# A linear-recurrence layer feeding a top-2 mixture of attention experts: a planner that prefers the present tiling, full-width gate matmuls, corrected planner costs, and a last unit that ends in two groups of query tiles

## The chip, the cores and the metric

The kernel runs on one core of a Trainium2 chip. The metric is device time in microseconds for one execution. Three executions before the change took 398.37, 399.69 and 401.26 us; their median, 399.69 us, is the time before. The execution that was profiled took 402.58 us, and its span, from the first to the last instruction, is 400.8 us.

## The reference

There are two layers. The first is a linear recurrence over 4 batches, 8 heads, 768 positions and head width 48. For each head, with a state of 48 x 48 that starts at zero:

```
cur   = outer(u * k[t], v[t])
y[t]  = r[t] @ (state + cur)
state = w[t][:, None] * state + outer(k[t], v[t])
```

Its output, with the heads side by side, is x of shape 4 x 768 x 384. The second layer takes x through four attention experts of head width 64, of which each position uses the two with the largest gate logits:

```
logits = x @ w_gate                      # 4 experts
w      = softmax over the 2 largest      # others weigh 0
for e in experts:
    q, k, v = x @ wq[e], x @ wk[e], x @ wv[e]
    a   = causal softmax(q @ k.T / 8)
    out += w[:, e] * (a @ v @ wo[e])
```

Every expert is computed for every position, and the weight of an expert that was not chosen is zero. The sharp scores (wq and wk are drawn with a large factor) are why products of q and k are split into a high and a low part and computed in three matmuls.

## The kernel before, in words

The work is cut into 8 units: batch b (4) times half g of the sequence (2), so a unit is 384 positions, which are 3 tiles of 128. A unit has a recurrence part, written by rwkv, and an attention part, written by moe.

**Recurrence.** Two heads are processed together, so a unit has 4 head pairs. The sequence is cut into chunks of 64. For a pair, VectorE runs scans over the decays (suf, pre), products go to GpSimd or VectorE (kt, mr, uk, ur), TensorE transposes kt (ktp, three 128x128 transposes) and multiplies in quarters of its array: aps (24 matmuls of 64x64), ups (state increments), and yps (outputs). VectorE scans over the chunk states (ys), masks aps into am, and adds yps to xn. One pair's ux step (line 409 on ScalarE) adds the u term, as three ScalarE instructions of 48 columns for each head.

**Attention.** xn is transposed (xp) and split into xh and xl. proj writes queries and keys of two experts at once (tile pp), vproj values and gate logits (vp). scores writes the scores of one query tile i for the two experts of a pair ep (tile sp), with the causal mask added by small matmuls; then come a maximum on VectorE (mx, line 650), an exponential on ScalarE (a, line 652), transposes on TensorE (tp, line 666), copies to ATa and ATb, and attend multiplies by the values (yp, line 689). gather computes the gates (gg on VectorE, then four GpSimd instructions that split them in three bf16 parts, a transpose gp, a copy gT); weigh spreads them over rows by a matmul with sel (gb) and multiplies; project_out multiplies by wo (op, line 758), copies (ob) and stores.

**Tilings.** A matmul uses the whole array of 128x128 (ktp, xp, pp, vp, tp, op), quarters of it (aps, ups, yps: mode "q"), two halves by rows (sp, and gb: mode "r") or two halves by columns (yp, and gp: mode "h").

**Order.** Nothing is issued in the order in which it is written. Every piece goes to Plan.add with the engines that may run it and a cost for each, the tiles that it reads and writes, and a wish time (want: the unit's start plus progress plus an offset for its kind from the table OFF, or OFF0 for the first unit). Plan.order then simulates all engines and picks, for each, among the ready pieces the one with the smallest wish time, no later than SLACK = 125 ns after the earliest that could start. A matmul of another tiling than the last one is charged DRAIN = 100 ns. So costs and offsets alone set the order of each engine's instructions, and every engine then runs its list strictly in that order.

**PSUM.** Of 8 banks, the recurrence has two (tag rw), the attention tiles two (mo), and scores two double ones (sc), each wide enough for both experts of a query tile up to 512 keys, or for one expert of a longer one. In the last unit no recurrence is left, and mbank alternates between mo and rw (the flag spare). BUFS gives the number of buffers of each tile in SBUF; ob has 2. Line 798 adds matmuls on a constant tile (warm), 14 at the start and 80 to be put where TensorE has nothing else.

**The last unit's end.** Its second expert pair computes scores for query tiles 0, 1, 2 in turn (512, 640 and 768 keys), then attend over all three tiles, gather, weigh and project_out.

## Time and profile before

| | |
|---|---|
| median of 3 executions | 399.69 us |
| the profiled execution | 402.58 us |
| its span | 400.8 us |
| TensorE busy with matmuls | 378.7 us, 94% |
| VectorE busy | 310.2 us, 77% |
| ScalarE busy | 236.2 us, 59% |
| GpSimd busy | 141.0 us, 35% |
| mean granted TensorE clock | 0.986 |

Busy time is the time in which at least one instruction of the engine is under way; with pipelined matmuls a busy TensorE is not one at its peak. In the answers that are quoted below, PE is TensorE, PEld its weight loads, DVE VectorE, ACT ScalarE, POOL GpSimd and SP SyncE. A row of the timeline has the start in us, the length in us, the engine, the line, what it writes and reads, the shape and the count of instructions merged in it; in brackets stands how long the engine had been idle and what released it. An fp32 matmul (aps, ups, yps, yp) is recorded as two instructions. A row of a table by stages has the stage, its length, and for each engine the busy time with the count of instructions, then the granted TensorE clock (1.00 is full), the share of the DMA engines and GB/s.

### The profile page before, as it was taken

What the parts mean: (1) busy time and instruction counts of PE and PEld (TensorE: products, weight loads), DVE (VectorE), ACT (ScalarE), POOL (GpSimd) and SP (SyncE); (2) the same over time, 40 slices, a digit from 0 to 9 for tenths busy, and PEclk for the clock granted to TensorE, in tenths of its full rate; (3) what the DMA queues carried; (4) which work ended last, traced back from release to release, by engine and by line L of the source; (5) the groups of instructions that cost most, each with busy time, mean ns of one, the idle gap of its engine ahead of it and who ended that gap; (6) DMA issues with size and microseconds to landing.
All of it is one profiled execution on the core that took longest, in us unless ns stands there. A gap on an engine that the chain in (4) does not pass through costs nothing.

```text
span 400.8 us, 12723 instructions
## 1 busy us (share of the span) xinstructions
PE 378.7 (94%) x5228; PEld 289.9 (72%) x5238; DVE 310.2 (77%) x684; ACT 236.2 (59%) x672; POOL 141.0 (35%) x247
## 2 busy tenths in 40 slices
PE   8789999999999999999989999999999999999875
PEld 3465877788857688778848688788768877778553
DVE  7989988998998988888946897786987853474332
ACT  2564766845667575746746587557645644556532
POOL 4435555452344555532212436533424102011000
PEclk9999999999999999999989999999999999999979
DMA  7885353544425527055403534431302001001001
GB/s 259 333 294 185 120 168 109 189 135 137 148 76 158 180 83 222 12 186 177 122 1 117 142 103 131 168 122 61 106 16 61 2 2 61 2 0 61 2 0 59
DMA packets 18057, 45.17 MB, mean 113 GB/s; under 512 B 2000, under 2 KB 9424, under 8 KB 18000
## 3 DMA queue, kind: packets, MB, share of 16 engines
q1 hardware_dynamic: 18000, 44.37, 34.2%
q8 instruction: 41, 0.67, 0.7%
q14 instruction: 16, 0.13, 0.1%
HBM read 39.64 MB, written 4.72 MB: 111 GB/s over the span
## 4 chain that ended last, share of the span: by engine, by line
PE 70%; DVE 13%; ACT 8%; DMA 5%; issue 3%; POOL 0%; ACTq 0%; POOLq 0%; DVEq 0%
PE pp L548 11%; PE tp L666 10%; PE sp L636 9%; PE yp L689 8%; PE vp L571 5%; PE aps L435 5%; PE op L758 5%; PE yps L479 4%; ACT xn L409 3%; DVE mx L650 3%; ACT a L652 3%; DVE ys L457 2%; PE yps L482 2%; PE ups L449 2%; PE ktp L419 2%
## 5 line engine op out<-in xcount | busy, mean ns | idle before, releaser
L652 ACT ACTIVATE a<-sp,mx 128x128 f32<-128x128 f32 (+5 forms) x96 | 60.8, 636 | 37.4 <-DVE mx L650 29.9
L650 DVE TENSOR_REDUCE mx<-sp 128x1 f32<-128x128 f32 (+5 forms) x96 | 56.4, 615 | 18.3 <-PE sp L641 16.4
L666 PE MATMUL tp<-ident,a 128*128 128x128 f32 x336 | 59.6, 291 | 8.2 <-ACT a L652 4.4
L666 PEld LDWEIGHTS tp<-ident,a 128*128 128x128 f32 x336 | 38.1, 143 | 19.0 <-ACT a L652 7.3
L389 POOL TENSOR_TENSOR kt<-lt,suf 128x384 f32<-128x384 f32 x31 | 31.7, 1022 | 42.4 <-PE aps L435 20.7
L396 POOL TENSOR_TENSOR nat<-nat,u_sb 128x288 f32<-128x288 f32 x30 | 27.0, 901 | 49.9 <-DMA nat<-in_nat_dram 29.3
L409 ACT ACTIVATE xn<-nat,rk 128x48 f32<-128x48 f32 x138 | 34.5, 325 | 13.4 <-DVE rk L402 13.3
L226 ACT COPY ATa<-tp 128x512 f32<-128x512 f32 (+3 forms) x64 | 30.8, 486 | 18.5 <-PE tp L666 17.7
L689 PE MATMUL yp<-ATa,v_sb 128*64 128x384 f32 (+2 forms) x224 | 40.2, 476 | 0.2 <-DVE ATa L228 0.2
L548 PE MATMUL pp<-xh,wh_qk 128*128 128x384 f32 x96 | 38.3, 399 | 0.5 <-ACT ATa L226 0.2
L384 DVE TENSOR_TENSOR_SCAN pre<-lt,inv_pre 128x390 f32<-128x390 f32 x32 | 34.1, 1067 | 0.1
L457 DVE TENSOR_TENSOR_SCAN ys<-ust,wdec 112x384 f32<-112x384 f32 x32 | 32.3, 1011 | 1.4 <-ACT ust L226 0.8
L380 DVE TENSOR_TENSOR_SCAN suf<-lt,one_suf 128x390 f32<-128x390 f32 x32 | 32.0, 1004 | 1.8 <-DMA lt<-in_wkr_dram 1.2
L479 PE MATMUL yps<-ys,pre 64*64 64x48 f32 (+1 forms) x768 | 31.2, 262 | 1.5 <-DVE am L438 0.8
L548 PE MATMUL pp<-xh,wl_qk 128*128 128x384 f32 x96 | 32.3, 337 | 0.0
L548 PE MATMUL pp<-xl,wh_qk 128*128 128x384 f32 x96 | 32.3, 337 | 0.0
L391 POOL TENSOR_TENSOR pre<-lt,pre 128x384 f32<-128x384 f32 x21 | 22.2, 1056 | 27.1 <-DVE pre L384 13.6
L435 PEld LDWEIGHTS aps<-pre,kt 64*64 64x64 f32 x768 | 25.0, 134 | 7.4 <-issue 3.5
L435 PE MATMUL aps<-pre,kt 64*64 64x64 f32 x768 | 29.3, 222 | 0.9 <-ACT kts L226 0.4
L387 ACT COPY wdec<-suf 128x288 f32<-128x288 f32 x32 | 22.6, 706 | 12.4 <-DVE suf L380 7.9
L479 PEld LDWEIGHTS yps<-ys,pre 64*64 64x64 f32 (+1 forms) x768 | 21.3, 133 | 10.0 <-issue 3.7
L482 PE MATMUL yps<-vy,am 64*64 64x48 f32 x768 | 28.2, 219 | 0.0
(135 smaller groups left out, 938.5 us busy)
## 6 DMA issues: line engine op xcount, KB each, us to landing
lt<-in_wkr_dram SPq DMA_DIRECT2D x31, 579.5 KB, 4.2
nat<-in_nat_dram SPq DMA_DIRECT2D x32, 432.0 KB, 3.8
vy<-in_vY_dram SPq DMA_DIRECT2D x32, 144.0 KB, 2.6
out_dram<-ob SPq DMA_DIRECT2D x24, 192.0 KB, 1.9
w_qk<-in_wqk_dram SPq DMA_DIRECT2D x1, 768.0 KB, 8.2
w_vg<-in_wvg_dram SPq DMA_DIRECT2D x1, 390.0 KB, 8.8
lt<-in_wkr_dram SPq DMA_DIRECT2D x1, 384.0 KB, 5.3
w_o<-in_wo_dram SPq DMA_DIRECT2D x1, 384.0 KB, 8.4
```

The source lines that it names most:

```text
L384: plan.add("pre", {"DVE": t_scan(WB)}, lambda e, pre=pre, w_=w_: nc.vector.tensor_tensor_scan(flat(pre()), w_()[:, 0:WB - 1], flat(inv_pre ...
L409: nc.scalar.mul(xn()[:, i, o], v[:, i, :], rk()[:, i, h:h + 1])
L435: nc.tensor.matmul(a_[half(h), c * C:(c + 1) * C], k[half(h), c, :], m[half(h), c, 0:C], start=True, stop=True)
L457: plan.add("ys", {"DVE": t_scan(D * NX)}, lambda e, ys=ys, us=us, wd=wd: nc.vector.tensor_tensor_scan(flat(ys()[0:112]), flat(us[0:112]), ...
L479: nc.tensor.matmul(yps[h]()[half(q), o], pre()[r, c, 0:C], ys()[r, :, c], start=i == 0, stop=False)
L482: nc.tensor.matmul(yps[h]()[half(q), o], am()[half(h), c, :], vy()[half(h), c, :], start=False, stop=i == 2)
L548: nc.tensor.matmul(pp()[:, 0:384], w[:, qk, k, cs], x()[:, k, :], start=(k == j == 0), stop=(k == j == 2))
L636: nc.tensor.matmul(spv(x)[:, h, :], q()[p, t], flat(k())[p, o], start=j == 0, stop=j == 2 and h < np_ - 1)
L650: plan.add("max", {"DVE": t_dve(n)}, lambda e, x=x, mx=mx: nc.vector.tensor_reduce(mx(), spv(x), axis=AX.XY, op=ALU.max, negate=True), [sp ...
L652: plan.add("exp", {"ACT": t_exp(n)}, lambda e, x=x, y=y, mx=mx, a=a: nc.scalar.activation(a()[:, 0:n].rearrange("p (a n) -> p a n", a=np_) ...
L666: nc.tensor.transpose(tp()[:, j * 128:(j + 1) * 128], a()[:, (j0 + j) * 128:(j0 + j + 1) * 128], ident)
L689: nc.tensor.matmul(yp()[e * 64:e * 64 + 64, lo:384], v_sb[ep]()[:, j, e * 64:e * 64 + 64], at, start=(j == 0), stop=(j == nj - 1))
```

## The change

The change has six parts, all in one edit.

1. In Plan.order, for TensorE alone, a piece of the present tiling has its wish time lowered by STAY = 2.0 us when the next piece is chosen, and the search among candidates goes on until the wish time is more than STAY past the first one's.
2. The gate matmuls are padded to the whole array: sel, gT and the gate tile have 128 rows or columns in place of 36, gp and gb get no tiling mode of their own, and gather clears the padded tile with a GpSimd memset.
3. Costs that the planner uses are changed: a ux on ScalarE from 273 to 675 ns, two GpSimd steps of the gates from 1300 and 700 to 1440 and 875 ns, the GpSimd step of gather from 1000 to 1290 ns.
4. In the last unit (batch 3, second half) scores with up to 512 keys go to the two banks of the recurrence, one for each expert.
5. In the last unit the second expert pair takes its query tiles in the order 1, 0, 2; attend, gather, weigh run for tiles 0 and 1 first and then for tile 2, and project_out of a tile reads only its group.
6. ob has 3 buffers in place of 2, and the tables of offsets (OFF, OFF0, MV, LEAD, T0, T1) have new numbers throughout.

The diff, cut; of the tables only three lines are shown:

```diff
@@ Plan.order
-                        if t <= free[e]:
+                        if t <= free[e] and (e != "PE" or want > c[0][1] + STAY):
                             break
...
-                want, n, t = min((x[1], x[2], x[0]) for x in c if x[0] <= t0 + slack)
+                want, n, t = min((x[1] - (STAY if e == "PE" and ops[x[2]]["mode"] == tiling else 0.0), x[2], x[0])
+                                 for x in c if x[0] <= t0 + slack)
@@ rwkv_moe
+    GROWS, GCOLS, GMODE = 128, 128, (None, None)
...
-    sel = cst.tile([NG, 3 * E, HD], BF16, name="sel")
+    sel = cst.tile([128, 3 * E, HD], BF16, name="sel")
...
-                plan.add("ux", dict(prod(144), ACT=3 * t_act(48)) if UXA else prod(144), ux, [(na, 0), rk], [(xn, p, h)])
+                plan.add("ux", dict(prod(144), ACT=675) if UXA else prod(144), ux, [(na, 0), rk], [(xn, p, h)])
@@ scores
-            sps = [bank("sc", f"sp{n0}{ep}{i}{a}", whole=np_ == 2) for a in range(np_)]
+            free = spare[0] and np_ == 1
+            sps = [bank("rw" if free else "sc", f"sp{n0}{ep}{i}{a}", whole=free or np_ == 2) for a in range(2 if free else np_)]
@@ attend, gather, weigh
+        last = (b, g) == (B - 1, 1)
+
+        groups = [(0, 2), (2, 3)] if last else [(0, 3)]
+
+        def attend(ep, ATs, i0, i1):
+
+            yp = mbank(f"yp{n0}{ep}{i0}")
+            nj = 3 * g + i1
             for j in range(nj):
...
+                ia = max(i0, j - 3 * g)
+                lo, hi = ia * 128, i1 * 128
...
+                gf = gg()[:, t].rearrange("p i e -> p (i e)")
+                a, b, c = (g3()[:, x * 3 * E + i0 * E:x * 3 * E + i1 * E] for x in range(3))
+                if GCOLS > NG or i1 - i0 < 3:
+                    V.memset(g3(), 0.0)
...
+            plan.add("g4", {"POOL": 1290}, parts, [gg], [gg, g3])
+            plan.add("gp", {"PE": 60}, lambda e: nc.tensor.transpose(gp()[0:GROWS, 0:128], g3(), identb), [g3], [gp], mode=GMODE[0])
+            plan.add("gT", {"DVE": 131}, lambda e: nc.vector.tensor_copy(gT(), gp()[0:GROWS, 0:128]), [gp], [gT])
...
+            plan.add("gb", {"PE": 56 * (i1 - i0)}, mm, [gT], [gb], mode=GMODE[1])
@@ moe
-            for i in range(3):
+            for i in (1, 0, 2) if last and ep else range(3):
...
+        for x, (i0, i1) in enumerate(groups):
+            gT = gather(i0, i1)
+            for ep in range(2):
+                weigh(ep, yps[ep][x if ep else 0], gT, i0, i1, *outs[ep])
+            for i in range(i0, i1):
+                project_out(i, [o[1:] for o in outs], i0)
@@ tables
-MV = {0: 27.58, 1: 45.34}
+MV = {0: 27.66, 1: 46.39}
...
+STAY = 2.0
...
-T0, T1 = (17.33, 15.85)
+T0, T1 = (21.06, 16.77)
```

Three places show how the instructions move. The first is TensorE's list in the second unit's attention, where two head pairs of the third unit's recurrence are woven in. ktp are the transposes of kt, aps and ups quarter-array work of the recurrence, tp the transposes of exponentials, sp scores. Before:

```order
L419 MATMUL ktp_1716<-ident,kt_1622 128x128 x3
L435 MATMUL aps_1724<-pre_1652,kt_1622 64x64 x12
L666 MATMUL tp_1746<-ident,a_1712 128x128 x4
L666 MATMUL tp_1760<-ident,a_1721 128x128 x4
L449 MATMUL ups_1767<-nat_1259,kts_1738 64x48
```

After:

```order
L421 MATMUL ktp_1716<-ident,kt_1603 128x128 x3
L437 MATMUL aps_1721<-pre_1628,kt_1603 64x64 x12
L437 MATMUL aps_1746<-pre_1699,kt_1676 64x64 x12
L671 MATMUL tp_1763<-ident,a_1738 128x128 x4
L421 MATMUL ktp_1770<-ident,kt_1676 128x128 x3
L671 MATMUL tp_1782<-ident,a_1761 128x128 x4
L641 MATMUL sp_1796<-Kh_700,Qh_1423 128x320
```

Two quarter-array pieces now stand one behind the other, and three whole-array pieces behind them, where before whole and quarter pieces took turns.

The second place is TensorE at the program's end, between the scores of the last unit's second expert pair and its attention. Before, with sp_6491 the scores of query tile 2 (768 keys) of the second expert:

```order
L641 MATMUL sp_6491<-causal,idh 128x128
L666 MATMUL tp_6517<-ident,a_6513 128x128 x4
L666 MATMUL tp_6522<-ident,a_6513 128x128 x2
L666 MATMUL tp_6527<-ident,a_6515 128x128 x4
L666 MATMUL tp_6536<-ident,a_6515 128x128 x2
L689 MATMUL yp_6546<-ATa_6441,v_sb_5829 64x384
```

After, with sp_6474 the scores of query tile 0 (512 keys), whose transposes read a_6492 and a_6501, and a_6488 and a_6512 the exponentials of query tile 2:

```order
L646 MATMUL sp_6474<-causal,idh 128x128
L671 MATMUL tp_6494<-ident,a_6488 128x128 x4
L671 MATMUL tp_6503<-ident,a_6492 128x128 x4
L671 MATMUL tp_6509<-ident,a_6488 128x128 x2
L671 MATMUL tp_6514<-ident,a_6501 128x128 x4
L671 MATMUL tp_6522<-ident,a_6512 128x128 x4
L671 MATMUL tp_6531<-ident,a_6512 128x128 x2
L699 MATMUL yp_6535<-ATa_6444,v_sb_5786 64x256
```

The scores of tile 2 (sp_6452 and sp_6454) now stand directly ahead of those of tile 0, so the transposes of both tiles share one stretch, and the scores that stood apart are two stretches (tile 1, then tiles 2 and 0) in place of three.

The third place is VectorE's list over the same stretch. Before, with mx the maxima, tile 2's alone:

```order
L650 TENSOR_REDUCE mx_6509<-sp_6489 128x1
L650 TENSOR_REDUCE mx_6511<-sp_6491 128x1
L228 COPY ATa_6441<-tp_6517 128x4x128
L706 SCALAR_TENSOR_TENSOR gg_6532<-asum_6175,gs_6302 128x12
L708 RECIPROCAL gg_6532<-gg_6532 128x12
```

After:

```order
L655 TENSOR_REDUCE mx_6484<-sp_6452 128x1
L655 TENSOR_REDUCE mx_6486<-sp_6472 128x1
L655 TENSOR_REDUCE mx_6490<-sp_6474 128x1
L655 TENSOR_REDUCE mx_6499<-sp_6454 128x1
L229 COPY ATa_6444<-tp_6494 128x4x128
L229 COPY ATa_6444<-tp_6503 128x4x128
L229 COPY ATb_6446<-tp_6509 128x256
L716 SCALAR_TENSOR_TENSOR gg_6527<-asum_6218,gs_6350 128x8
```

Four maxima of two query tiles stand together, those of tile 0 between the two of tile 2, and three copies stand between them and the first group's gates.

More of the change, by code (lines that the diff above doesn't have):

```diff
@@ L602, in ranks @@
                 V.tensor_tensor(rank(), c2()[:, :, :, 0], c2()[:, :, :, 1], op=ALU.add)
-            plan.add("gate", {"POOL": 1300}, ranks, lgk + ["masks", m1], [c1, c2, rank, ge])
+            plan.add("gate", {"POOL": 1440}, ranks, lgk + ["masks", m1], [c1, c2, rank, ge])
             plan.add("gate", {"ACT": 250}, lambda e: nc.scalar.activation(ge(), ge(), AF.Exp), [ge], [ge])
@@ L611, in norm @@
                 V.tensor_scalar(gs(), gs(), 1e-9, None, op0=ALU.add)
-            plan.add("gate", {"POOL": 700}, norm, [ge, c1], [gs, c1])
+            plan.add("gate", {"POOL": 875}, norm, [ge, c1], [gs, c1])
         def scores(ep, i):
@@ L690, in mm @@
                                          at, start=(j == 0), stop=(j == nj - 1))
-                step(2 * 0.9 * (384 - lo) / 1000)
-                plan.add("av", {"PE": 2 * 0.905 * (384 - lo) + 4}, mm,
-                         [(v_sb[ep], j)] + [(ATs[e][jj], i) for e in range(2) for i in range(3) for jj in range(g + 1)
+                step(2 * 0.9 * (hi - lo) / 1000)
+                plan.add("av", {"PE": 2 * 0.905 * (hi - lo) + 4}, mm,
+                         [(v_sb[ep], j)] + [(ATs[e][jj], i) for e in range(2) for i in range(i0, i1) for jj in range(g + 1)
@@ L705, in over @@
             def over(e):
-                nc.vector.scalar_tensor_tensor(gg(), asum(), 1e-9, gs()[:, :, None].to_broadcast([128, 3, E]),
+                nc.vector.scalar_tensor_tensor(gg()[:, t], asum()[:, t], 1e-9, gs()[:, t, None].to_broadcast([128, i1 - i0, E]),
                                                op0=ALU.add, op1=ALU.mult)
-                nc.vector.reciprocal(gg(), gg())
-                nc.vector.tensor_tensor(gg(), gg(), ge(), op=ALU.mult)
-            plan.add("g3", {"DVE": 640}, over, [(asum, i, x) for i in range(3) for x in range(E)] + [ge, gs], [gg])
+                nc.vector.reciprocal(gg()[:, t], gg()[:, t])
@@ L712, in parts @@
+                nc.vector.tensor_tensor(gg()[:, t], gg()[:, t], ge()[:, t], op=ALU.mult)
+            plan.add("g3", {"DVE": 640}, over, [(asum, i, x) for i in range(i0, i1) for x in range(E)] + [ge, gs], [gg])
             def parts(e):
                 V = nc.gpsimd
-                gf = gg().rearrange("p i e -> p (i e)")
-                V.tensor_copy(g3()[:, 0, :], gf)
-                V.tensor_tensor(gf, gf, g3()[:, 0, :], op=ALU.subtract)
-                V.tensor_copy(g3()[:, 1, :], gf)
@@ L758, in mm @@
                         nc.tensor.matmul(op()[:, 0:DM], y()[:, t], w[:, ep, :], start=(j + ep == 0), stop=(j == 2 and ep == 1))
[L759 removed]
+                plan.add("op", {"PE": 3 * 172}, mm, [(y, i0) for pair in parts for y in pair] + [("wh", "o", 0), ("wl", "o", 0)] + ([op] if ep else []), [op])
             ob = sb([128, DM], F32, "ob", f"ob{n0}{i}")
@@ L778, in moe @@
                     transposes(ATs[e], a, 2 * ep + e, i)
-            yps.append(attend(ep, ATs))
-        gather()
-        parts = [weigh(ep, yps[ep]) for ep in range(2)]
-        for i in range(3):
-            project_out(i, parts)
+            yps.append([attend(ep, ATs, *t) for t in (groups if ep else [(0, 3)])])
+        outs = [(sb([128, 384], F32, "yr", f"yr{n0}{ep}"), sb([128, 384], F32R, f"yh{ep}", f"yh{n0}{ep}"),
+                 sb([128, 384], F32R, f"yl{ep}", f"yl{n0}{ep}")) for ep in range(2)]
+        for ep in range(2):
+            yr = outs[ep][0]
+            if not (LATE and ep == 1 and spare[0]):
+                plan.add("yr", {"ACT": t_act(384)}, lambda e, yp=yps[ep][0], yr=yr: nc.scalar.copy(yr(), yp()[:, 0:384]),
+                         [yps[ep][0]], [yr])
+        for x, (i0, i1) in enumerate(groups):
+            gT = gather(i0, i1)
+            for ep in range(2):
+                weigh(ep, yps[ep][x if ep else 0], gT, i0, i1, *outs[ep])
+            for i in range(i0, i1):
+                project_out(i, [o[1:] for o in outs], i0)
     units = [(b, g) for b in range(B) for g in range(2)]
```

76 lines of the change are left out of this document (34 added, 42 removed).

## The prediction

> **What bounds the kernel now.** I read the page first, then the busy time by stages of 20 us, then TensorE's waits, then the last 31 us instruction by instruction.
>
> ```profile
> span 400.8 us, 12723 instructions
> PE 378.7 (94%) x5228; PEld 289.9 (72%) x5238; DVE 310.2 (77%) x684; ACT 236.2 (59%) x672; POOL 141.0 (35%) x247
> ...
> 40.00:60.00 20.00, 19.67 (x338) 16.91 (x339) 18.53 (x38) 13.63 (x47) 10.56 (x14) 1.00 0.42 143
> 100.00:120.00 20.00, 18.81 (x262) 14.05 (x260) 19.49 (x37) 13.34 (x36) 7.86 (x12) 1.00 0.36 115
> 380.00:401.00 21.00, 14.10 (x80) 9.99 (x78) 6.08 (x13) 6.31 (x13) 0.80 (x4) 0.83 0.08 29
> ```
>
> TensorE bounds all but the two ends: it is busy 19.67 of 20 us at 40, with VectorE close behind (19.49 of 20 at 100). In the last stage it is busy 14.10 of 21 us, and its clock is down to 0.83. So the change can gain in two ways: less TensorE time in the middle, or a shorter end.
>
> ```profile
> PE tp L666 <- ACT a L652: 4.4, 4, 2.1
> ...
> 202.00:204.00 2.00, 0.73 (x6) 0.39 (x4) 2.00 (x5) 0.69 (x2) 0.39 (x1) 1.00 0.00 0
> 204.00:206.00 2.00, 2.00 (x16) 1.02 (x16) 1.72 (x4) 1.05 (x4) 0.00 (x0) 0.71 0.00 0
> 206.00:208.00 2.00, 2.00 (x10) 0.79 (x8) 0.74 (x3) 1.24 (x3) 0.00 (x0) 0.50 0.00 0
> 208.00:210.00 2.00, 2.00 (x18) 0.94 (x14) 0.00 (x0) 0.21 (x2) 0.00 (x0) 0.93 0.00 0
> ...
> 376.00:378.00 2.00, 0.59 (x12) 0.31 (x8) 1.56 (x3) 0.46 (x1) 0.00 (x0) 1.00 0.00 0
> 380.00:382.00 2.00, 2.00 (x13) 1.67 (x13) 0.29 (x1) 0.59 (x1) 0.00 (x0) 0.50 0.03 8
> 386.00:388.00 2.00, 2.00 (x9) 1.55 (x10) 1.20 (x5) 0.79 (x2) 0.79 (x4) 0.50 0.00 0
> ```
>
> The largest wait is the transposes' on the exponentials (4.4 us in four pieces), and two of the pieces are in the end. Each hole has a second price behind it: after TensorE idled at 376 the clock stands at 0.50 at 380, and at 386 again, behind a second hole. After the stage at 202, where 0.73 of 2 us were busy, it stands at 0.71, 0.50 and 0.93: 0.58 + 1.00 + 0.14 = 1.7 us of clock lost, or some 3.4 us at half. So a hole of 1.3 us or more costs its own length and then up to 1.7 us of TensorE work.
>
> **The preference for the present tiling.** Counting neighbouring matmuls of different tiling over the whole of TensorE's order, there are 307 changes before and 286 after; in the last stretch 10 before and 14 after, so elsewhere 25 fewer. One change has a price that these rows show:
>
> ```profile
> 151.06 0.33 PE L758 MATMUL op<-wl_o,yh 128*128 128x384 f32 x1
> 151.23 0.33 PE L758 MATMUL op<-wh_o,yl 128*128 128x384 f32 x1
> 151.49 0.25 PE L449 MATMUL ups<-nat,kts 64*64 64x48 f32 x1
> ...
> 156.07 0.30 PE L482 MATMUL yps<-vy,am 64*64 64x48 f32 x8
> 156.19 0.36 PE L479 MATMUL yps<-ys,pre 64*64 64x48 f32 x8
> 156.35 0.31 PE L482 MATMUL yps<-vy,am 64*64 64x48 f32 x8
> 156.59 0.44 PE L548 MATMUL pp<-xh,wh_qk 128*128 128x384 f32 x1
> 156.87 0.34 PE L548 MATMUL pp<-xh,wl_qk 128*128 128x384 f32 x1
> ```
>
> Within op the next matmul starts 0.17 us later (151.06 to 151.23), across the change into quarters 0.26: 0.09 more. Eight matmuls of L482 take 0.12 us (156.07 to 156.19), but the change back takes 0.24 (156.35 to 156.59): 0.12 more. I take 0.10 for each: 25 x 0.10 = 2.5 us. If the slow first step of pp (0.28 us) belonged to the change too, 0.11 more on each second change, the mean would be 0.16 and the sum 4.0; if TensorE waits for VectorE at the places where changes go, nothing is gained. So 0 to 4.0, and 2.5 taken, because TensorE has under 4% of slack in the middle stages.
>
> The preference has a price that no row shows: work of another tiling whose wish is up to 2 us earlier stands back. Where it feeds VectorE's scans this delays a chain that is nearly full. I charge nothing in the sum and give it a rival.
>
> **Padded gates.** gp and gb stream the same number of columns as before, so TensorE's time is the same to either side of 0.1 us; the 12-column work of GpSimd gets one memset per gather more, nine in all, beside an engine at 35%. In the last unit the memset needs no gate and can run while GpSimd waits. Nothing.
>
> **Real costs.** The ux step's row in the groups of the page:
>
> ```profile
> L409 ACT ACTIVATE xn<-nat,rk 128x48 f32<-128x48 f32 x138 | 34.5, 325 | 13.4 <-DVE rk L402 13.3
> ```
>
> The true cost of a ux on ScalarE is three times 34.5/138 = 0.75 us; the planner believed 0.27 and now believes 0.675. Its order follows the chip better: in the order after, 117 such instructions (39 ux of 64) stand on ScalarE, before 138 (46). VectorE takes over some of ScalarE's and GpSimd's pieces, five more ob copies among them, a few us on its 310. Whether a hole such as that at 202 goes or a new one comes cannot be read from the order; in the sum 0, in the range one hole either way: 1.5 idle + 1.7 of clock = 3.2 us.
>
> **Start.** The first pp stands behind 86 warm matmuls in place of 88, and one nat transfer ahead of a larger lt. Two matmuls of 512 columns take, by the 0.17 us of the 384 columns of op above, about 0.5 us. 0 taken, 0.5 either way.
>
> **The end.** Before, it lasts from the first scores of the second expert pair at 369.65 to 400.8: 31.15 us. These are its prices:
>
> ```profile
> 369.65 0.50 PE L636 MATMUL sp<-Kh,Qh 64*128 64x512 f32 x2
> 370.91 2.80 PE L689 MATMUL yp<-ATa,v_sb 128*64 128x384 f32 x16
> 371.02 1.29 DVE L650 TENSOR_REDUCE mx<-sp 128x1 f32<-128x512 f32 x2 [0.95 <-PE sp L641]
> 372.41 0.69 ACT L652 ACTIVATE a<-sp,mx 128x512 f32<-128x512 f32 x1 [2.01 <-DVE mx L650]
> 374.29 1.09 PE L666 MATMUL tp<-ident,a 128*128 128x128 f32 x8
> 375.32 0.42 PE L636 MATMUL sp<-Kh,Qh 64*128 64x320 f32 x2
> 376.62 1.55 DVE L650 TENSOR_REDUCE mx<-sp 128x1 f32<-128x640 f32 x2 [0.44 <-PE sp L641]
> ...
> 378.48 2.10 PE L666 MATMUL tp<-ident,a 128*128 128x128 f32 x10 [1.89 <-ACT a L652]
> 382.82 1.82 DVE L650 TENSOR_REDUCE mx<-sp 128x1 f32<-128x768 f32 x2 [1.84 <-PE sp L641]
> 383.87 0.90 ACT L652 ACTIVATE a<-sp,mx 128x768 f32<-128x768 f32 x1 [2.83 <-DVE mx L650]
> 384.92 2.42 PE L666 MATMUL tp<-ident,a 128*128 128x128 f32 x12 [2.13 <-ACT a L652]
> 386.22 0.16 DVE L706 SCALAR_TENSOR_TENSOR gg<-asum,gs 128x12 f32<-128x12 f32 x1
> 387.81 0.21 POOL L718 TENSOR_TENSOR g<-gg,g 128x12 bf16<-128x12 f32 x1
> ...
> 392.32 0.44 PE L758 MATMUL op<-wh_o,yh 128*128 128x384 f32 x1
> 396.39 0.33 PE L758 MATMUL op<-wh_o,yl 128*128 128x384 f32 x1
> 397.10 0.48 ACT L226 COPY ob<-op 128x384 f32<-128x384 f32 x1 [0.91 <-DMA out_dram<-ob]
> ```
>
> Scores of 640 keys take 1.3 us (375.32 to 376.62). For 768 I take 1.3 x 768/640, about 1.5 at full clock; for 512 about 1.1 (1.26 from 369.65 to 370.91, some of it a wait). yp of the first pair takes 3.4 (370.91 to 374.29), a transpose 0.13 (1.03 for eight).
>
> After, counted from the first scores of the second pair:
> - Scores of tile 1 to 1.5 (their first step waits for Kl as now). While VectorE and ScalarE make its exponentials (1.55 and then 0.8, ready at 4.2), TensorE does yp of the first pair, to 4.9. This cover is what the new order brings; the hole of 1.89 us is gone. Transposes of tile 1 to 6.2.
> - Scores of tile 2 to 7.6, at once those of tile 0, in the freed banks, to 8.6.
> - VectorE: maxima of 0.91, 0.65, 0.65 and 0.91 from 7.6. ScalarE: exponentials of 0.90, 0.69, 0.69 and 0.90 from 8.6, done at 9.5, 10.2, 10.9 and 11.8. TensorE idles from 8.6 to 9.6, then does the 20 transposes (2.6 us) in pieces behind the exponentials, to about 12.6, with 0.5 of gaps.
> - Attention of both groups streams as many columns as before (4 x 384 + 256 + 128 = 1920 for an expert; 4 x 256 + 128 and then 6 x 128 also make 1920): 3.4. Gates of the first group (1.8 on VectorE and GpSimd, 386.22 to 388.02) lie beside it; two gp, six gb and eight changes add about 1.5. The first group's last yl is ready at about 17.6.
> - 18 op x 0.175 = 3.15, from 17.7 to 20.9. In the order all op still stand behind the last yp, so splitting brings no earlier op; it takes the first group's multiplications out of the chain, and the second group's (ready at 18.8) lie beside the first op.
> - From there to the end before: 400.8 - 396.72 = 4.1 us, of which 0.2 was the third ob's wait for a buffer that a store held; with three buffers 3.9. Sum: 24.9.
>
> So at full clock 31.15 - 24.9 = 6.25 us less. But from 8.6 to 12.6 TensorE idles about 1.5 us in pieces, more than the 1.27 us of the stage at 202 (2.00 - 0.73), and there the clock fell. I take one drop: 1.7 us of the transposes and yp behind it. The end then gives 4.6 us.
>
> [...]
>
> **Sum.** 2.5 + 4.6 = 7.1 us. The profiled execution took 402.58, so 395.5; it lies 2.9 above the median, and against the median 399.69 - 7.1 = 392.6 us.
>
> **Rivals.**
> - The clock holds in the end: 1.7 more, 390.9. For it: the hole is 1.0 us in place of 1.9 and 2.1, and transposes run between. Against it: the drop after 202. Chance 0.17.
> - The plan with true costs has no hole like that at 202, and the rest as forecast: 3.2 more, 389.4. Chance 0.13.
> - The middle gives nothing and gains a hole: TensorE waits for VectorE where changes were saved, since VectorE has 19.49 of 20 us at 100 and takes over ScalarE's copies. 2.5 lost and 3.2 more lost: 398.3; without the hole 395.1. The band from 395.7 to 402 has 0.24, about 397.5.
> - Slower: the preference holds aps, ups or yps back while VectorE is full, in the first 140 us. VectorE cannot make up what it loses there, and about half of the 32 head pairs, with three such pieces each, stand in that stretch. Each delay of 1.5 us that lands on an empty VectorE is 1.5 us on the end; five use up the gain, and eight (12 us) give about 405. Against it: rows show VectorE's queue nearly always full of other work. Chance 0.06.
> - That the change doesn't do what it says is excluded for its main part: the count of changes is lower and the scores stand as described. For early projection it is so, and the sum has none.
>
> My forecast as stated has the remaining 0.40, with 390.5 to 395.0 for its own range.
>
> **Range and chances.** Two repeats differ by up to 0.7%, so under 1%, 4.0 us, counts as no change: faster is below 395.7. Faster: 0.17 + 0.13 + 0.38 = 0.68. The same: 0.02 + 0.24 = 0.26. Slower: 0.06. The range 388.0 to 399.0 leaves out 0.06 above as slower, 0.05 of the third rival and 0.05 of the second.
>
> **What would show it.** In the end: from the first scores of 640 keys to the last instruction, 25 us at full clock, 26.6 with one drop; one wait of tp for an exponential near 1.0 us in place of 1.89 and 2.13; no [DMA out_dram<-ob] ahead of the last ob. In the middle: a TensorE sum about 2.5 us smaller and stages still over 19.5 of 20. I would be wrong if the holes between 40 and 360 us grow by more than 3 us or if the end has two drops of the clock again.

## The result, and the profile after

The changed kernel takes 385.27 us (median of four executions, 385.02 to 385.49); the kernel before, measured beside it, 399.59. The ratio is 0.9639 with a 95% interval of 0.9603 to 0.9675: 14.3 us less, where 7.1 were forecast, and below the range. The profiled execution took 385.41 us, its span is 383.6; before they were 402.58 and 400.8, so these two executions differ by 17.2 us.

First the page of the changed kernel (span and engines), then its stages up to and from the first scores of the last expert pair, and the same two stages of the kernel before:

```profile
span 383.6 us, 12786 instructions
PE 370.9 (97%) x5259; PEld 287.9 (75%) x5259; DVE 314.0 (82%) x703; ACT 230.7 (60%) x646; POOL 150.3 (39%) x264
```

```profile
0.00:359.49 359.49, 351.67 (x5093) 274.25 (x5093) 302.42 (x675) 218.82 (x619) 148.60 (x255) 1.00 0.39 124
359.49:383.60 24.11, 19.28 (x167) 13.62 (x166) 11.58 (x29) 11.83 (x28) 1.71 (x9) 0.98 0.07 25
```

```profile
0.00:369.65 369.65, 356.13 (x5085) 274.57 (x5095) 299.86 (x665) 224.37 (x647) 140.16 (x243) 1.00 0.38 121
369.65:400.80 31.15, 22.56 (x146) 15.36 (x145) 10.33 (x20) 11.81 (x26) 0.80 (x4) 0.87 0.05 19
```

The 17.2 us are 31.15 - 24.11 = 7.0 in the end and 369.65 - 359.49 = 10.2 ahead of it. Of the 10.2, TensorE's idle time gives 13.52 - 7.82 = 5.7 and its busy time 4.5; 1.7 of that is the clock lost behind the hole at 202, so 2.8 remain. That is about what the changes of tiling were forecast at, but the two stages do not show that it is them. (Ten TensorE records are missing from the trace of before; by an estimate from 356.13 us of busy time for 5085 records, 0.07 each, 0.7 us of its idle time may be work.) Most of the 10.2 us is won before the last unit's attention begins. The row of the last unit's input transposes has first and last start; before, then after:

```profile
L502 PE MATMUL xp<-ident,xn x72: 270/273/329, 28.1 to 336.8; 128*128 128x128 f32 x72
```

```profile
L504 PE MATMUL xp<-ident,xn x72: 270/272/331, 25.2 to 327.2; 128*128 128x128 f32 x72
```

The last one starts 9.6 us earlier. The stage of 20 us that holds the former hole at 202 is now full:

```profile
200.00:220.00 20.00, 20.00 (x311) 15.26 (x307) 16.37 (x32) 13.72 (x33) 4.64 (x9) 1.00 0.36 114
```

TensorE's timeline in the end of the changed kernel, and the last copies on ScalarE:

```profile
359.49 0.41 PE L641 MATMUL sp<-Kh,Qh 64*128 64x320 f32 x2
360.70 2.80 PE L699 MATMUL yp<-ATa,v_sb 128*64 128x384 f32 x16
364.08 1.31 PE L671 MATMUL tp<-ident,a 128*128 128x128 f32 x10
365.32 0.44 PE L641 MATMUL sp<-Kh,Qh 64*128 64x384 f32 x2
366.58 0.48 PE L641 MATMUL sp<-Kh,Qh 64*128 64x512 f32 x2
368.85 1.99 PE L671 MATMUL tp<-ident,a 128*128 128x128 f32 x14 [1.19 <-ACT a L657]
371.07 0.87 PE L671 MATMUL tp<-ident,a 128*128 128x128 f32 x6 [0.23 <-ACT a L657]
371.87 1.95 PE L699 MATMUL yp<-ATa,v_sb 128*64 128x256 f32 x16
373.75 0.23 PE L733 MATMUL gp<-identb,g 128*128 128x128 bf16 x1
373.91 0.44 PE L699 MATMUL yp<-ATb,v_sb 128*64 128x128 f32 x4
...
376.81 0.44 PE L767 MATMUL op<-wh_o,yh 128*128 128x384 f32 x1
379.86 0.34 PE L767 MATMUL op<-wh_o,yl 128*128 128x384 f32 x1
```

```profile
380.24 0.48 ACT L227 COPY ob<-op 128x384 f32<-128x384 f32 x1 [0.56 <-PE op L767]
```

The transposes of tile 1 start at once behind yp; one wait for exponentials is left, 1.19 us (and 0.23), in place of 1.89 and 2.13; the last ob waits for TensorE and no longer for a store. The clock stays at 1.00 up to the last matmul (mean of 359.49 to 380.20).

### The profile page after: what moved, and what is told of

The parts are those of the page before. It is cut to its first block, busy times and chain, and to the rows that moved or that the text cites. A ratio compares the mean times of both kernels' runs of the same rounds, so it can differ in the third digit from the quotient of the medians.

```text
span 383.6 us, 12786 instructions
## 1 busy us (share of the span) xinstructions
PE 370.9 (97%) x5259; PEld 287.9 (75%) x5259; DVE 314.0 (82%) x703; ACT 230.7 (60%) x646; POOL 150.3 (39%) x264
## 4 chain that ended last, share of the span: by engine, by line
PE 75%; DVE 14%; ACT 4%; issue 2%; DMA 2%; POOL 1%; SPq 0%; ACTq 0%; DVEq 0%; POOLq 0%
PE pp L550 11%; PE tp L671 9%; PE yp L699 9%; PE sp L641 9%; PE op L767 7%; PE vp L573 7%; PE aps L437 6%; PE yps L481 4%; PE ups L451 2%; PE ktp L421 2%; DVE mx L655 2%; PE yps L484 2%; DVE suf L382 2%; PE warm L816 2%; ACT a L657 2%
## 5 line engine op out<-in xcount | busy, mean ns | idle before, releaser
L655 DVE TENSOR_REDUCE mx<-sp 128x1 f32<-128x128 f32 (+5 forms) x96 | 56.5, 615 | 14.5 <-PE sp L646 12.7
L671 PE MATMUL tp<-ident,a 128*128 128x128 f32 x336 | 56.3, 283 | 3.0 <-ACT a L657 1.4
L227 ACT COPY ATa<-tp 128x512 f32<-128x512 f32 (+3 forms) x66 | 32.2, 496 | 20.2 <-PE tp L671 19.7
L391 POOL TENSOR_TENSOR kt<-lt,suf 128x384 f32<-128x384 f32 x28 | 27.5, 981 | 42.9 <-PE aps L437 16.3
L398 POOL TENSOR_TENSOR nat<-nat,u_sb 128x288 f32<-128x288 f32 x30 | 28.9, 963 | 27.7 <-DMA nat<-in_nat_dram 19.7
L699 PE MATMUL yp<-ATa,v_sb 128*64 128x384 f32 (+2 forms) x240 | 38.3, 435 | 0.0
L550 PE MATMUL pp<-xh,wh_qk 128*128 128x384 f32 x96 | 37.1, 387 | 0.0
L411 ACT ACTIVATE xn<-nat,rk 128x48 f32<-128x48 f32 x117 | 29.9, 327 | 10.4 <-DVE rk L404 10.2
L382 DVE TENSOR_TENSOR_SCAN suf<-lt,one_suf 128x390 f32<-128x390 f32 x32 | 34.2, 1072 | 1.3 <-DMA lt<-in_wkr_dram 1.2
L459 DVE TENSOR_TENSOR_SCAN ys<-ust,wdec 112x384 f32<-112x384 f32 x32 | 30.3, 951 | 2.1 <-ACT ust L227 1.3
L816 PE MATMUL warm<-one_suf 128*128 128x512 bf16 x94 | 27.1, 417 | 1.4 <-POOL one_suf L247 1.4
## 6 DMA issues: line engine op xcount, KB each, us to landing
lt<-in_wkr_dram SPq DMA_DIRECT2D x1, 384.0 KB, 5.3
w_o<-in_wo_dram SPq DMA_DIRECT2D x1, 384.0 KB, 8.6
```

Source lines behind the costliest of these rows:

```text
L227: nc.scalar.copy(o, i)
L382: plan.add("suf", {"DVE": t_scan(WB)}, lambda e, suf=suf, w_=w_: nc.vector.tensor_tensor_scan(rev(suf()), rev(w_()), rev(one_suf), 0.0, op ...
L550: nc.tensor.matmul(pp()[:, 0:384], w[:, qk, k, cs], x()[:, k, :], start=(k == j == 0), stop=(k == j == 2))
L655: plan.add("max", {"DVE": t_dve(n)}, lambda e, x=x, mx=mx: nc.vector.tensor_reduce(mx(), spv(x), axis=AX.XY, op=ALU.max, negate=True), [sp ...
L671: nc.tensor.transpose(tp()[:, j * 128:(j + 1) * 128], a()[:, (j0 + j) * 128:(j0 + j + 1) * 128], ident)
L699: nc.tensor.matmul(yp()[e * 64:e * 64 + 64, lo:hi], v_sb[ep]()[:, j, e * 64:e * 64 + 64], at, start=(j == 0), stop=(j == nj - 1))
```

## The experiments

### One part undone in the changed kernel

Old end:

```diff
-        groups = [(0, 2), (2, 3)] if last else [(0, 3)]
+        groups = [(0, 3)]
-            for i in (1, 0, 2) if last and ep else range(3):
+            for i in range(3):
-            free = spare[0] and np_ == 1
+            free = False
```

> The changed kernel with the last unit's end as before: query tiles 0, 1, 2 in turn, one group, all scores in the banks sc. Everything else, the tables too, is as after; in the list of TensorE there are 287 changes of tiling against 286. If the new end is worth what the two traces show from the first scores of the second expert pair (31.15 us before, 24.1 after), this kernel takes 385.3 + 6 to 7 = 391.5 to 392.5 us, the first scores of the pair stand within 1 us of 359.5, and the clock falls in the end once or twice again. Rival: the new tables alone make the end short, and tile order and groups are worth only the split of a chain: 386 to 388 us.

Measured: 392.39 us (391.28 to 394.10), 7.1 more than the changed kernel. In its profile the last xp and the first scores of the second pair stand within 1 us of where they stand after the change (the scores at 358.93), so in the changed kernel the end is worth 7 us, a slow stretch of the clock in it included (0.50 from 370.06 to 373.47), and the rest of the gain lies ahead of it.

No preference:

```diff
-                        if t <= free[e] and (e != "PE" or want > c[0][1] + STAY):
+                        if t <= free[e]:
-                want, n, t = min((x[1] - (STAY if e == "PE" and ops[x[2]]["mode"] == tiling else 0.0), x[2], x[0])
+                want, n, t = min((x[1] - 0.0, x[2], x[0])
```

> The changed kernel without the preference for the present tiling (the wish is not lowered, and the search ends where it did before); the order of all engines changes with it, and TensorE has 314 changes of tiling in place of 286. If the preference is worth its changes of tiling at 0.10 us, 28 of them: 2.8 us more, 388 us, with 1.5 us either way for the other order. Rival: the preference makes the whole gain of 10 us ahead of the end (369.65 to 359.49): 394 to 396 us. Second rival: TensorE waits elsewhere what it saves: 385 to 386 us.

Measured: 395.55 us (395.27 to 396.74), 10.3 more, as the first rival had it. Its page:

```profile
PE 376.6 (96%) x5252; PEld 288.0 (73%) x5259; DVE 316.2 (80%) x729; ACT 220.7 (56%) x600; POOL 151.6 (39%) x268
```

TensorE is busy 5.7 us longer, which is 0.20 us for each of the 28 further changes, and idle 17.0 us (393.6 - 376.6) in place of 12.7 (383.6 - 370.9), 4.3 longer.

Old tables (OFF, OFF0, MV, LEAD, T0 and T1 of before), and old costs:

```diff
-                plan.add("ux", dict(prod(144), ACT=675) if UXA else prod(144), ux, ...
+                plan.add("ux", dict(prod(144), ACT=3 * t_act(48)) if UXA else prod(144), ux, ...
```

with 1300, 700 and 1000 ns for the GpSimd steps again.

> The changed kernel with the offsets and starts of before (OFF, OFF0, MV, LEAD, T0, T1); preference, gates, costs and end as after; 292 changes of tiling. If the tables carry what TensorE's idle time lost ahead of the end (13.5 us before, 7.8 after, 2.5 of it in the first 40 us) and the clock lost after the hole at 202 (1.7 us): 385.3 + 5 to 7 = 390 to 392.5 us. Rival: preference and true costs made the order good whatever the tables: 385 to 387 us.

> The changed kernel with the costs of before in the planner (ux on ScalarE 273 ns, the GpSimd steps of the gates 1300, 700 and 1000 ns); 291 changes of tiling. If true costs only shift work among engines that have slack, as the sum took them, the time is within 1.5 us of 385.3 us. Rival: they are what removed the hole at 202 and the idle time between 40 and 360 us; then holes come back, 385.3 + 3 to 6 = 388.5 to 391 us.

Measured: 390.68 us with the old tables, 5.4 more, as expected; 399.95 us (398.75 to 401.32) with the old costs, 14.7 more, far beyond both expectations. With the old costs TensorE waits in stages that are full in the changed kernel (first the old costs, then the changed kernel):

```profile
20.00:40.00 20.00, 17.11 (x334) 11.29 (x340) 14.26 (x32) 9.61 (x33) 10.56 (x13) 1.00 0.72 239
60.00:80.00 20.00, 16.86 (x303) 12.66 (x300) 17.73 (x38) 14.51 (x49) 11.06 (x18) 1.00 0.52 169
```

```profile
20.00:40.00 20.00, 19.95 (x329) 12.49 (x328) 18.55 (x39) 9.26 (x29) 12.29 (x12) 1.00 0.74 240
60.00:80.00 20.00, 19.94 (x345) 14.65 (x345) 18.60 (x40) 14.40 (x46) 12.71 (x20) 1.00 0.52 152
```

The four parts together cost 37.5 us when each is undone by itself; the whole change is worth 14.3. So these are not prices of parts.

### What a small disturbance costs

In the changed kernel, one number each (two kernels):

```diff
-dict(prod(144), ACT=675)
+dict(prod(144), ACT=685)
```

```diff
-STAY = 2.0
+STAY = 1.9
```

> The changed kernel with one of the planner's costs moved by 1.5%: ux on ScalarE 685 ns in place of 675. The work is the same, but the order is another one from the middle on (290 changes of tiling against 286). If the gain of 10 us ahead of the end belongs to what the edits do (preference, true costs), such a step costs nothing: 385.3 within 1.5 us. Rival: the costs, the preference and the tables together hit one good order, which any disturbance loses: 388 to 394 us, by TensorE's idle time and not by its work; then what single undone parts cost (10.3 without the preference, 14.7 with the old costs) is mostly the loss of this order.

> The changed kernel with STAY 1.9 in place of 2.0 us; the order differs from the middle on (297 changes of tiling against 286). As a robust effect, 11 changes at 0.13 to 0.17 us make it 1.5 to 2 us longer: 387 us. Rival as for the cost moved by 1.5%: a lost order, 389 to 395 us.

Measured: 387.81 us (387.35 to 387.89) and 387.56 us (387.28 to 387.85), 2.5 and 2.3 more. For STAY the time is what 11 further changes were expected to cost. For the cost, it lies between the two expectations: 4 changes at the 0.13 us that is measured below explain 0.5 us, and TensorE's idle time grew from 12.7 to 16.7 us (386.1 - 369.4; 11 of its records are missing there, 0.8 us at the 0.07 estimated above), so most of the loss is waiting.

In the kernel before, nothing but

```diff
-yl0=1, yl1=1, ob=2,
+yl0=1, yl1=1, ob=3,
```

> The kernel before with three buffers of ob in place of two and nothing else; the work is the same, but the order differs from the second unit on (314 changes of tiling against 307). If the tables of before fit one order, and any disturbance loses it: 3 to 8 us more, 403 to 408 us. Rival: the buffers are neutral, 7 changes at 0.13 to 0.17: 400 to 401 us.

Measured: 404.84 us (404.16 to 405.23) beside 400.08: 4.8 us slower, with no work changed and a buffer more. The order of before was fitted to its tables too.

### One part alone in the kernel before

Of the change's diff the lines in Plan.order, with three buffers of ob (the expectation leaves them out); the tables with three buffers; the lines on scores, groups and the order of query tiles with three buffers, and with two:

> The kernel before with the preference alone (STAY 2.0 and the longer search); tables, costs, gates and end as before; 298 changes of tiling against 307. As a robust effect of fewer changes: 9 at 0.13 to 0.17, 1.2 to 1.5 us less, 398.4 us. If the preference is worth what its removal cost in the changed kernel (10.3 us): 389.5 us. If every disturbance of a fitted order loses some us: 401 to 406 us.

> The kernel before with the new tables (OFF, OFF0, MV, LEAD, T0, T1) and three buffers of ob alone: no preference, old costs, unpadded gates, old end; 319 changes of tiling. If the tables carry the middle's gain by themselves: 392 to 394 us. If they fit only together with the preference and the true costs: no gain, 400 us or more.

> The kernel before with the new end alone (scores in the recurrence's banks, tile order 1, 0, 2, two groups, three buffers of ob); tables, costs, gates and choice among candidates as before; 323 changes of tiling. If the end is worth its 6.5 to 7 us by itself: 399.8 - 6.5 = 393 us, within 1.5 us for the order that it disturbs. Rival: without the new tables the end's pieces are not in the new order, and it gains 2 to 4 us only.

> The kernel before with the new end alone and two buffers of ob: all engines' lists are word for word those of before up to the last unit's end (TensorE's first 2507 rows), which the end with three buffers was not. If the end is worth by itself what it was in the changed kernel: 7 us less than before, 392.5 to 393.5 us. Rival: part of the 7 us came with the tables: 395 to 397 us.

| in the kernel before | us | before beside it |
|---|---|---|
| the third ob alone (above) | 404.84 | 400.08 |
| the preference, three ob | 400.80 | 399.82 |
| the new tables, three ob | 412.84 | 400.08 |
| the new end, three ob | 401.83 | 399.82 |
| the new end, two ob | 395.81 | 400.08 |

All but the last have the third buffer, so they are to be read against the third buffer alone. Against it the preference gains about 4 us (397.07 to 401.57 against 404.16 to 405.23; 298 changes of tiling in place of 314), and the new tables lose 8. The runs of the preference and of the buffer alone were not made side by side, and the preference with two buffers was not run, nor the true costs alone. The new end with three buffers is 3.0 us faster than the third buffer alone; VectorE's first 646 instructions, up to 355 us, are the same in both. With two buffers, where the order ahead of it is that of before (VectorE's first 643 instructions, up to 352 us), it gains 4.3. The end alone was expected at 7; it is 3 to 4.3, as the rival had it. Where its yp of the first pair stands differs with the tables:

```profile
371.27 0.45 PE L550 MATMUL pp<-xh,wh_qk 128*128 128x384 f32 x1
372.01 0.44 PE L699 MATMUL yp<-ATb,v_sb 128*64 128x128 f32 x4
372.38 0.42 PE L641 MATMUL sp<-Kh,Qh 64*128 64x320 f32 x2
375.76 1.43 PE L671 MATMUL tp<-ident,a 128*128 128x128 f32 x8 [0.96 <-ACT a L657]
```

With the old tables yp is done before the scores, between pieces of pp, and covers no exponentials (this is the kernel with two buffers); the cover that the prediction counted on came with the new tables.

### The clock

Two holes of before filled (ahead of tile 1's and tile 2's first transpose; the bank is the transposes' own):

```diff
                 def tr(e, tp=tp, j0=j0, nj=nj):
+                    if (b, g) == (B - 1, 1) and x == 2 and j0 == 0 and i > 0:
+                        z = one_suf.bitcast(BF16)
+                        for _ in range(4 + i):
+                            nc.tensor.matmul(tp()[:, 0:512], z[:, 0:128], z[:, 0:512], start=True, stop=True)
```

> The kernel before with five and six matmuls of 512 columns on a constant tile put into TensorE's two waits for exponentials in the last unit's end (1.89 and 2.13 us), ahead of the first transpose of query tiles 1 and 2; they write the bank that the transposes then overwrite. The order and the lengths of the waits of other engines are as before. Theory: each wait keeps only about 0.8 us of idle time, the clock holds at 1.00 behind both, and the kernel gains up to 2 x 1.7 = 3.4 us against before, at least 2. Rival: TensorE is not what the end waits for, so clock or no clock it stays within 0.7 us of before.

The new rows of the first hole (one of its five matmuls is missing from the trace):

```profile
374.75 1.03 PE L668 MATMUL tp<-one_suf 128*128 128x512 bf16 x4 [0.16 <-issue]
376.49 1.54 PE L670 MATMUL tp<-ident,a 128*128 128x128 f32 x10 [0.71 <-ACT a L652]
```

Measured: 397.81 us against 399.79 (ratio 0.9952, 0.9933 to 0.9971): useless matmuls make the kernel 2.0 us faster, the least that was expected. In all twelve executions the mean clock is 0.998 to 1.000, although the hole at 202 was not filled.

The executions of the kernel before fall in groups by their mean clock: 18 with 0.985 to 0.987 take 401.2 us on the mean, 32 with 0.989 to 0.991 take 400.4, 18 with 0.994 to 0.996 take 398.8 (one more has 0.981 and takes 402.1). One stretch of 3.41 us at half is 1.7 of 400, 0.004 of the mean clock, so by this working, without a trace of each, a group has three, two or one of them, and the filled kernel none. From 401.2 to 397.8 in three steps (0.8, 1.6 and 1.0) that is about 1.1 us each, less than the 1.7 that was taken. The profiled execution of before had three.

In it the granted clock is 0.50 from 204.85 to 208.26, from 378.93 to 382.34 and from 385.76 to 389.17. The starts of these slow stretches, and TensorE's busy time in the 3.41 us ahead of each:

```profile
201.44:204.85 3.41, 1.87 (x13) 1.11 (x12) 3.29 (x6) 1.93 (x7) 0.95 (x2) 1.00 0.00 0
375.52:378.93 3.41, 1.52 (x20) 1.24 (x19) 2.22 (x3) 1.44 (x4) 0.00 (x0) 1.00 0.00 0
382.35:385.76 3.41, 1.27 (x14) 0.76 (x10) 1.97 (x3) 1.87 (x4) 0.00 (x0) 1.00 0.00 0
...
204.80:204.90 0.10, 0.10 (x4) 0.04 (x3) 0.10 (x2) 0.10 (x2) 0.00 (x0) 0.76 0.00 0
378.90:378.95 0.05, 0.05 (x3) 0.05 (x1) 0.00 (x0) 0.05 (x1) 0.00 (x0) 0.81 0.00 0
385.75:385.80 0.05, 0.04 (x1) 0.00 (x1) 0.05 (x1) 0.00 (x0) 0.00 (x0) 0.57 0.00 0
399.40:399.45 0.05, 0.00 (x0) 0.00 (x0) 0.00 (x0) 0.00 (x0) 0.00 (x0) 0.61 0.00 0
```

The clock turns at 204.85, 378.93, 385.76 and 399.41 (behind the last matmul): the distances, 174.08, 6.83 and 13.65 us, are 51, 2 and 4 times 3.413. So in this execution the four turns lie on a grid of 3.413 us. The theory was that there is such a grid in every execution, and that TensorE's busy time between two of its lines decides whether a slow stretch follows. After the change the clock turned once, after the end (0.59 in the mean of 382.60 to 383.60, so 0.82 us ahead of its end, at 382.78); five and four steps of 3.413 back from it, where lines would stand by the theory, are 365.72 and 369.13, and the window between them holds the 1.19 us:

```profile
365.72:369.13 3.41, 2.22 (x29) 1.57 (x26) 2.32 (x5) 1.57 (x4) 0.00 (x0) 1.00 0.02 5
```

2.22 us busy, and the clock held, which fits the theory. A longer hole was made by two exponentials more on ScalarE:

```diff
+                        for _ in range(2):
+                            nc.scalar.activation(spent, one_suf[:, 0:384], AF.Exp, bias=mx())
```

> The changed kernel with two more exponentials of 384 columns (results unused) on ScalarE ahead of query tile 2's first exponential in the last unit, so that TensorE's wait of 1.19 us for it grows by about 1.2 us to 2.4; the order is the same. Theory (idle time counts by a fixed grid of 3.41 us: 1.19 us in one window left the clock at 1.00 after the change, 1.52 us in one window took it down before): the clock falls to 0.50 for 3.41 us behind the hole in most of the executions, those in which the grid does not cut the hole in two, and these take 385.3 + 1.2 + 1.7 = 388.2 us, the others 386.5 us. Rival (such gaps don't cost the clock, what fell before had another cause): all executions 386.5 us, the clock 1.00 throughout.

Measured: 386.49 us (385.78 to 386.99). Two of four executions have a mean clock of 0.994 and take 386.63 and 386.99, the other two 1.000 and 385.78 and 386.34. The profiled one is of the latter (385.05:385.15 lies behind its last instruction):

```profile
369.76 1.99 PE L680 MATMUL tp<-ident,a 128*128 128x128 f32 x14 [2.34 <-ACT a L666]
...
368.03:371.44 3.41, 1.67 (x13) 1.40 (x14) 2.56 (x5) 3.38 (x9) 0.00 (x0) 1.00 0.00 0
385.05:385.15 0.10, 0.00 (x0) 0.00 (x0) 0.00 (x0) 0.00 (x0) 0.00 (x0) 0.72 0.00 0
```

So with this longer hole (2.34 us in the profile) the clock fell in two executions of four, by their mean clocks, and not in the two others; no trace shows where it fell. That "most" would lose it was too much, and the loss is 0.75 us on the mean of two and two executions (386.81 against 386.06), not 1.7. The clock turns at 385.09, so four and five steps back the theory has lines at 371.44 and 368.03. The second cuts the hole (367.42 to 369.76), but the window behind it still holds 1.74 us of idle time, more than the 1.54 ahead of the slow stretch at 204.85, and the clock held. (The 1.52 us of the expectation is a busy time; the idle time of the windows that fell before the change was 1.54 to 2.14.) In the changed kernel with the old end, whose clock turns at 370.06, the two waits for exponentials, 1.89 and 2.13 us, went both ways in one execution:

```profile
366.64:370.06 3.42, 1.52 (x17) 1.08 (x14) 1.85 (x3) 2.15 (x5) 0.00 (x0) 1.00 0.00 0
370.06:373.47 3.41, 2.99 (x20) 2.09 (x17) 0.68 (x2) 0.66 (x2) 0.00 (x0) 0.50 0.02 5
373.47:376.88 3.41, 1.69 (x13) 1.29 (x13) 2.41 (x5) 2.37 (x6) 0.00 (x0) 1.00 0.00 0
```

Behind the window with 1.52 us busy the clock fell, behind the one with 1.69 it stayed at 1.00, and before the change it fell behind 1.87. So a grid is shown for the turns of one execution, and the theory is not: TensorE's busy time in a window, as the profile has it, does not alone decide, and what does stays open.

### The price of a change of tiling

```diff
+                        if i and ep == 0 and j == 0:
+                            r = slice(0, 128 if i == 1 else 64)
+                            nc.tensor.matmul(op()[r, 384:432], yh()[r, t][:, r], w[r, ep, 0:48], start=True, stop=True)
```

> The changed kernel with one more matmul of 48 columns ahead of op of query tile 1 (full width, 128x128) and of query tile 2 (64x64, a quarter of the array) in each unit; its result is overwritten. It measures one change of tiling and back by itself, where op of the tiles stand one behind the other. Taken in the prediction: 0.10 us for each change, so the quarter matmul costs 0.2 us more than the full one. Rival: the first step of what follows is slower too (0.28 in place of 0.17 us), 0.2 us a change: 0.4 us more.

Measured: 387.85 us (one execution), 2.6 more than the changed kernel for 16 matmuls. The price is read from the rows:

```profile
265.85 0.34 PE L770 MATMUL op<-wh_o,yl 128*128 128x384 f32 x1
266.02 0.18 PE L769 MATMUL op<-wh_o,yh 128*128 128x48 f32 x1
266.05 0.42 PE L770 MATMUL op<-wh_o,yh 128*128 128x384 f32 x1
266.31 0.34 PE L770 MATMUL op<-wl_o,yh 128*128 128x384 f32 x1
...
267.00 0.34 PE L770 MATMUL op<-wh_o,yl 128*128 128x384 f32 x1
267.27 0.23 PE L769 MATMUL op<-wh_o,yh 64*64 64x48 f32 x1
267.44 0.44 PE L770 MATMUL op<-wh_o,yh 128*128 128x384 f32 x1
267.72 0.33 PE L770 MATMUL op<-wl_o,yh 128*128 128x384 f32 x1
```

From the last matmul of a tile to the second of the next it takes 0.46 us with the full-width matmul between (265.85 to 266.31) and 0.72 with the quarter one (267.00 to 267.72): 0.26 for two changes, 0.13 each. The slow first step (0.26 and 0.28 in place of 0.17) comes behind the matmul of 48 columns at either width, so it does not come with the tiling. By 0.13, the 25 changes saved are 3.3 us; the two stages above left 2.8. Only changes between the whole array and quarters were measured.

### The padded gates

The changed kernel with sel, gT and the gate tile at 36, in the same order:

```diff
-    GROWS, GCOLS, GMODE = 128, 128, (None, None)
+    GROWS, GCOLS, GMODE = NG, NG, (None, None)
```

> The changed kernel with sel, gT and the gate tile of 36 rows or columns as before, gp and gb so unpadded, but ordered as after (the planner still takes them for full-width); no memset where a unit has one group. The prediction took the padding at nothing: 385.3 within 0.5 us. Rivals: the unpadded matmuls cost their changes of tiling (gp and gb, 8 + 17 places, up to two changes each at 0.10 us, less those that stand together): 387 to 389 us; or the padded transpose gp, whose share of TensorE's list grew from 0.27 to 1.43 us in all, is dearer: 384.2 us.

Measured: 383.69 us (383.04 to 384.44). Single executions of one order differ by some tenths of a us (385.02 to 385.49 for the changed kernel), so this kernel and the changed one were run side by side:

> The changed kernel itself, beside the one with unpadded gate tiles. 385.0 to 385.5 us as before, if its times are as close together on every chip; up to 386.5 us if executions differ more than the first four showed.

> The kernel with unpadded gate tiles in the order of the changed one. If the padding costs TensorE time: 1.2 to 2.0 us less than the changed kernel beside it. If the difference was one of executions: within 0.5 us of it.

384.93 us (384.37 to 385.06) padded, 383.96 (383.48 to 384.62) unpadded: 1.0 us less without the padding. In the end of the unpadded kernel:

```profile
370.86 1.95 PE L699 MATMUL yp<-ATa,v_sb 128*64 128x256 f32 x16
372.64 0.22 PE L733 MATMUL gp<-identb,g 128*36 128x128 bf16 x1
372.65 0.43 PE L699 MATMUL yp<-ATb,v_sb 128*64 128x128 f32 x4
...
375.31 0.44 PE L767 MATMUL op<-wh_o,yh 128*128 128x384 f32 x1
```

From 36 columns the next yp starts 0.01 us behind gp (372.64 to 372.65), from 128 columns 0.16 us (373.75 to 373.91), and the stretch from the first group's yp to the first op takes 4.45 us in place of 4.94. So the padding costs 1.0 us. That it does so as a change of tiling in the middle of yp is likely, but not shown apart from the width of gp itself; gb and the memset changed with it.

### A filled hole

The unpadded kernel, with the last keys of the first pair's yp put off to the hole of 1.19 us (in attend):

```diff
-                         [...] + ([yp] if j else []), [yp], mode="h")
+                         [...] + ([yp] if j else []), [yp], mode="h",
+                         want=plan.now + 14.0 if last and ep == 0 and j >= 4 else None)
```

> The changed kernel with unpadded gate tiles (order as after), and in the last unit the keys from 512 on of the first expert pair's yp wished 14 us after the pair's time in the plan, so that they stand behind the scores of query tile 2, where TensorE waited 1.19 us. If that fills the hole: 383.7 - 0.7 to 1.2 = 382.5 to 383 us. Rival: the tiles that are held longer put the transposes and maxima later by as much: 383.5 to 385 us.

Measured: 384.84 us (384.29 to 385.38), the time of the rival. The largest wait for exponentials fell to 0.50 us, but the new wish moved more than yp: both exponentials of tile 2 now stand ahead of those of tile 0. So whether held banks or this order cost what the cover gives is not shown. The fastest version that was run is the changed kernel with unpadded gate tiles, at 383.7 to 384.0 us; it beats both kernels.

## Why the prediction was wrong

- **What bounds.** Right: TensorE, with holes in the end and at 202 and the clock behind them.
- **The preference, 2.5 us.** The price of a change was close, 0.10 taken and 0.13 measured, so 25 of them make 3.3 us, and the two stages leave 2.8. But the changes saved are not what the preference is worth: 10.3 us in the changed kernel, and about 4 in the one before with a third buffer of ob.
- **Padded gates, nothing.** Off by 1.0 us to the slower side. Columns streamed were counted and they are the same; that they alone set the time was the author's assumption, which no run shows. In the ends of the two kernels yp goes on 0.01 us after the start of a transpose of 36 columns and 0.16 us after that of one of 128.
- **Real costs, 0 with 3.2 either way.** This is the step that failed. It set the middle's idle time to stay, because it "cannot be read from the order". It fell by 5.7 us with the start's share, and in the profiled executions the clock loss of 1.7 behind 202 went too: 7.4 us of the 17.2, where the range allowed 3.2. Part of it is in the first 40 us, which had a term of their own, "0 taken, 0.5 either way": TensorE's busy time there went from 16.05 and 18.48 in two stages of 20 us to 17.06 and 19.95. No single part owns this gain: undone by itself, the preference costs 10.3 us, the true costs 14.7 and the new tables 5.4, together 30.4, where 10.2 were won ahead of the end. So the parts fit each other, and the new tables without the others lose. The prediction has no term for the tables at all.
- **The end, 4.6 us.** The replay at full clock, 6.25, was close to the 7.0 that came: idle 1.5 forecast, 1.42 measured; first op at 17.7, measured 17.3 (376.81 - 359.49); from the last matmul to the end 3.9, measured 3.4 (383.6 - 380.2). The drop that was put on top did not come. Its ground, a stretch with 1.27 us idle that cost the clock, counted idle time by a stage of the table and not by the grid: the window that fell held 1.54 us of idle time (3.41 - 1.87), the one that held 1.19. The smaller idle time may be why, but windows with 1.72 and 1.74 us of it held too, so that a hole of 1.3 us or more costs the clock, as the prediction has it, is not so every time.
- **Rivals.** The two favourable ones, a clock that holds in the end (0.17) and no hole in the middle (0.13), both came true at once. They were priced as alternatives; together they give 392.6 - 1.7 - 3.2 = 387.7, and that case had no chance of its own and lay below the range. The 2.4 us from there to 385.3 had no term: of the 5.7 us of idle time that went, the one hole was priced at 1.5. The slower rival (VectorE starved in the first 140 us) is not to be seen: VectorE is busy 19.45 and 19.26 us of 20 in the two stages from 100 us, TensorE 19.47 and 19.35.
- **Execution and median.** The profiled execution of before had three slow stretches where, by the mean clock, 32 of 69 executions have two and 18 have one. That is part of why 17.2 us between the profiled executions are 14.3 between medians; the sum took clock losses from the one and subtracted them from the other. The loss behind 202 is of this kind: in the twelve executions with filled holes and the four with the new end and two buffers, whose order there is that of before, the mean clock is 0.998 or more.

What stays open is why the fitted order is the better one: no single wait was found that the new tables remove, only many short ones, and TensorE's work without the preference grows by more (5.7 us) than 28 changes at 0.13 explain.

## What to carry to other kernels

Where a planner sets the order, undoing one part of a change does not price that part, since costs, rules and offsets have been fitted to each other: an added buffer alone cost 4.8 us here, and new offsets together with it 12.8. Compare runs that differ in the one part only: read against the kernel before, the preference with the added buffer seems worth nothing, and read against the buffer alone, about 4 us. Price parts in a fixed order (the first 2507 rows of TensorE's list the same, or only a tile's width changed), and give the joint case of two favourable rivals its own chance. In the kernel with the longer hole the clock fell in two executions and held in the two others, so count the loss over many executions; and where a hole can't be closed, useless matmuls in it can pay, 2.0 us here.

## What was not expected of the hardware

By the groups of mean clocks, a slow stretch of 3.41 us cost about 1.1 us of the kernel and not 1.7, and their number varies from one execution to the next (mean clocks of 0.981 to 0.996 in 69 executions of before): the spread of before (397.3 to 402.8 us) is in part that, and after the change, with one hole of 1.19 us, four executions lie within 0.5 us. Behind a window with 1.74 us of idle time the clock held at 1.00, and behind one with 1.54 it was 0.50. Behind the start of a transpose of 36 columns between column-half matmuls the next matmul started after 0.01 us, behind one of 128 columns after 0.16.
